# GpSimd's last-level products of near tokens: eight instructions of 384 elements in place of two of 1536

## The chip, the cores and the metric

The kernel runs on one core of a Trainium2 chip. The metric is the device time of one execution in microseconds (us); the time of a kernel is the median of its runs. TensorE appears in the profile as PE (matmuls) and PEld (weight loads), VectorE as DVE, ScalarE as ACT, GpSimd as POOL, and SyncE, which issues most DMAs, as SP.

## The reference

Two blocks follow each other. The first is a recurrence over 768 tokens for 4 sequences and 8 heads of 48 dimensions; the second is a feed-forward block over the 3072 tokens that come out of it (384 to 2048 to 384 dimensions). All is float32.

```python
for t in range(S):
    cur = einsum('bhd,bhe->bhde', u[None] * k_t, v_t)
    y[:, :, t] = einsum('bhd,bhde->bhe', r_t, state + cur)
    state = w_t[..., None] * state + einsum('bhd,bhe->bhde', k_t, v_t)
h = x @ w_in                      # x: y with the heads side by side
g = h * erf(softplus(h))
out = g @ w_out
```

Token t thus sees every earlier token s with the weight (sum over d of r[t,d] k[s,d] times the product of w between them).

## The kernel before, in words

**Steps.** The work is cut into 12 steps (s = 0 to 11) of 2 sequences by 128 tokens by 8 heads. Within a step, the weights between tokens are found by levels: at level n, blocks of 2^n tokens are split in two halves, and each token of the right half meets each token of the left half. Levels 5 and 6 are matmuls (`level_products`). For steps 5 to 11 the levels 1 to 4, the "near" tokens within a block of 16, are done without TensorE: `prepare(s)` holds r, k and w of the step as rows (128 partitions, each one block of 16 tokens by 48 dimensions), multiplies r by k elementwise, and sums over the 48 dimensions.

**`prepare(s + 1)` runs inside step s.** It is a generator; `attend_late(s, ...)`, the body of steps 5 to 11, advances it piece by piece between its own instructions, and step 4 (`attend`) does so for step 5. So the near tokens of steps 5 to 11 are prepared in steps 4 to 10, seven times in all. The names in `prepare`: `multiply(engine, level)` forms the products of a level (lines 484 to 493), `fade` multiplies r or k by decays (line 462), `add_total` forms decays over longer stretches (line 455), `sum_up` sums products over the 48 dimensions on VectorE (line 528).

**Level 4** has 8 left tokens by 8 right tokens by 48 dimensions for each partition: 3072 products. `multiply_last(nc.gpsimd, part)` (line 502) forms them on GpSimd, half of the left tokens at a time. Part 0 goes into the buffer `front`, which the profile shows as `rk`; part 1 goes into `back`, shown as `words` (r and k themselves lie in a `words` buffer too). Part 1 takes the place of the products of level 3, so it comes behind `sum_up(3)`. After part 1, GpSimd fades k for the last time (`fade(nc.gpsimd, k, 4)`, line 462). VectorE sums the two parts much later in the step (`sum_up(4, 0)` and `sum_up(4, 1)`, line 528 with 1536 elements), and SyncE then writes the faded k and the sums to DRAM and reads them back in another order (`k_blocks`, `by_blocks`, `by_tokens`, `kT`).

**The order of the work is written out by hand.** All engines run under `manual_schedule`, each in program order. What goes between the pieces of a late step is a string of tokens; for steps 6 to 10 it is

```python
USUAL = (
    "s P", "m", "ey P m s P P ep P", "m k22y P F P k11p F", "S1", "S2 S3 H k12y S4 H F",
    "s H ey m H H F s H ep H H",
)
```

for the places "front", "near", 0, 1, 2, 3, 4. `P` is an eighth of the output product of step s - 3 (`project_fast`, matmuls of line 1212, then sums on VectorE in lines 1232 and 1237), `H` a piece of the hidden product of step s - 1 (`hidden`, matmuls of line 1097, copied out by ACT in line 1106), `s`, `e` and `m` are softplus, erf and the multiplication `h <- h * erf` (VectorE, line 1062), `F` advances `prepare(s + 1)`, and `S`, `k` blend tokens for a later `P`. Step 5 has a list of its own, in which the output product is `project` (line 1129).

On VectorE, in steps 6 to 10, this gives the following row around the two GpSimd instructions of line 502: `sum_up(2)` (line 528), a multiplication `m` (1062, `h<-h,pp`), `sum_up(3)` (528), `kT` times the spread decays (793), a second `m` (1062, `h<-h,y`), the scaling of `in` by decays for level 5 (`scale`, line 333, 512 elements), a third `m` (1062, `h<-h,pp`), the sum `o<-o,m` (1232), `scale` for level 6 (333, `in<-in,w`), the sum `o<-o,m` (1237), two further `scale` (333).

The matmuls of `P` and of `H` share two PSUM buffers `m`. The first `H` of a step writes into the buffer that the VectorE instruction of line 1232 reads last. On TensorE it comes behind `state_part` (line 734, `pp<-v,kT`), which in its turn is behind the last `P`.

Of the kernel before, what the change touches and what calls it, by code (L numbers as in the profile page):

```python
# [17 lines left out]
P = 128  # L18
# [28 lines left out]
def view(ap, offset, dims):  # L47

    return bass.AP(ap.tensor, ap.offset + offset, [ap.ap[0], *dims])
# [12 lines left out]
def kernel(  # L62
# [18 lines left out]
    NH, D = v.shape[2:]  # L81
# [277 lines left out]
    def prepare(s):  # L359
# [3 lines left out]
        if s < DIRECT:  # L363
            rk1 = att.tile([P, 2, JP, C], FP32, name="rk1", bufs=1)
            ready[s] = (rk1,)
            parts = 1 if s else NJ
# [56 lines left out]
        else:  # L423
            half = view(tots[NEAR_LOG + 1], 1, [[2, NC], [C >> NEAR_LOG + 1, JP]])
# [3 lines left out]
            to = over_blocks[:].rearrange("p (h b) n -> p b h n", h=NC)  # L428
# [5 lines left out]
        r, k, w = rows_of.pop(s)  # L434
# [32 lines left out]
        for level in (0, 1, 2, 3):  # L467
            half = 1 << level - 1 if level else 0
# [5 lines left out]
        half = 1 << NEAR_LOG - 1  # L474
        parts = [x[:, : half * half * D // 2] for x in (front, back)]
# [22 lines left out]
        def multiply_last(engine, part):  # L498

            rows = half // 2  # L500
            left = k[:, part * rows : (part + 1) * rows]
            engine.tensor_mul(  # L502
                parts[part].rearrange("p (s t d) -> p s t d", t=half, d=D),
                r[:, None, half:].to_broadcast([P, rows, half, D]),
                left[:, :, None, :].to_broadcast([P, rows, half, D]),
            )

        def sum_up(level, part=None):

# [39 lines left out]
        if levels == NEAR_LOG:  # L549
            fade(beside, k, 3)  # L550
            add_total(beside, 3)
            fade(nc.vector, r, 3)
            sum_up(2)
            multiply_last(nc.gpsimd, 0)
            yield
            sum_up(3)
            multiply_last(nc.gpsimd, 1)
            fade(nc.gpsimd, k, NEAR_LOG)
        else:
            yield  # L560
            sum_up(2)
            sum_up(3)
# [917 lines left out]
    for kk in range(KT):  # L1480
        n = D // KT
        to, of = (x.rearrange("p (e m) -> p e m", e=NE) for x in (apart[:, kk], ident[:]))
        nc.vector.tensor_copy(out=to[:, :, D:], in_=of[:, :, kk * n : (kk + 1) * n])
    load_first()
    with tc.manual_schedule(
# [74 lines left out]
        s = n_steps  # L1560
# [108 lines left out]
```

## Time and profile before

| What | Value |
|---|---|
| Median of 3 runs | 584.71 us (583.98 to 586.29) |
| The profiled execution | 582.61 us |
| its span | 580.8 us |
| granted TensorE clock | 1.0 |
| PE busy | 572.0 us (98%) |
| DVE busy | 435.8 us (75%) |
| ACT busy | 355.4 us (61%) |
| POOL busy | 226.5 us (39%) |
| line 502, part 0 | 7 instructions of 1536 elements, mean 3447 ns |
| line 502, part 1 | 7 instructions of 1536 elements, mean 4201 ns |

The profile is of one execution. Its span runs from the first to the last instruction; the rest of its time, 1.8 us, lies around the span. In the timeline each row has the start in us from the span's start, the duration in us, the engine, the line, the operation, the tile that is written and those that are read, the shape, and, in brackets, how long the engine was idle before and who released it. Rows of one engine overlap by up to 0.1 us, because an instruction is recorded from its own start to its last write. A step of the kind 6 to 10 takes 44.87 us; the examples below are mostly from step 6 (235.75 to 280.62 us).

### The profile page before, as it was taken

To read this page: it belongs to the slowest core of one execution; us is meant where nothing else is said; L and a number is where in the kernel's file an instruction comes from. 1 tells how busy PE (TensorE), PEld (TensorE's weight loads), DVE (VectorE), ACT (ScalarE), POOL (GpSimd) and SP (SyncE) were. 2 spreads that over 40 slices of the span, in tenths; PEclk is the share of its full clock that TensorE was granted. 3 is DMA by queue.
4 is the path that set the end of the run, shared out by engine and by line. 5 is a ranking of instruction groups with operands and counts; after the bars stand their busy time and mean duration, and the time that the engine had idled before them with its cause. 6 is when DMAs were issued, how large, how long until landed. Compare 5 with 4: busy or idle time off the path is not lost.

```text
span 580.8 us, 16457 instructions
## 1 busy us (share of the span) xinstructions
PE 572.0 (98%) x7240; PEld 491.4 (85%) x7240; DVE 435.8 (75%) x462; ACT 355.4 (61%) x478; POOL 226.5 (39%) x222
## 2 busy tenths in 40 slices
PE   8999999999999999999999999999999999999997
PEld 6688886688578668998998998998898899988997
DVE  8784866998895798798699599599599537256640
ACT  3768787554453797847747747756666761388700
POOL 4566481606764675373273183173172000000000
PEclk9999999999999999999999999999999999999999
DMA  7595753250352326136135235234232301000000
GB/s 259 194 359 197 249 191 139 101 151 7 140 193 56 107 75 168 18 138 183 30 132 183 39 133 183 39 123 150 47 110 81 47 8 37 1 1 2 28 27 28
DMA packets 54080, 63.23 MB, mean 109 GB/s; under 512 B 35160, under 2 KB 40568, under 8 KB 52984
## 3 DMA queue, kind: packets, MB, share of 16 engines
q1 hardware_dynamic: 53624, 61.98, 33.7%
q8 instruction: 57, 0.93, 0.7%
q10 hardware_dynamic: 384, 0.20, 0.1%
q14 instruction: 15, 0.12, 0.1%
HBM read 52.39 MB, written 8.69 MB: 105 GB/s over the span
## 4 chain that ended last, share of the span: by engine, by line
PE 70%; issue 12%; DVE 12%; POOL 4%; DMA 1%; ACT 1%; SPq 0%; DVEq 0%; POOLq 0%; ACTq 0%
PE m L1097 30%; PE m L1212 12%; PE m L1129 11%; PE pp L627 5%; PE pp L1300 4%; DVE h L1062 3%; PE y L1300 2%; DVE sums L528 2%; POOL words L462 2%; DVE in L333 2%; DVE words L493 2%; POOL own L455 1%; PE y L659 1%; PE pp L734 1%; PE y L685 1%
## 5 line engine op out<-in xcount | busy, mean ns | idle before, releaser
L1097 PE MATMUL m<-xT,w_in_sb 128*128 128x256 f32 x960 | 214.6, 382 | 2.5 <-DVE o L1232 2.5
L1097 PEld LDWEIGHTS m<-xT,w_in_sb 128*128 128x128 f32 x960 | 180.0, 190 | 28.0 <-DVE o L1232 3.2
L333 DVE TENSOR_TENSOR in<-in,tot_sb 128x1024 f32<-128x1024 f32 (+1 forms) x55 | 79.7, 1449 | 16.4 <-PE pp L627 15.1
L1106 ACT COPY h<-m 128x512 f32<-128x512 f32 x80 | 46.3, 580 | 52.3 <-PE m L1097 52.3
L1129 PE MATMUL m<-w_out_sb,h 128*128 128x384 f32 x192 | 64.3, 491 | 0.0
L1129 PEld LDWEIGHTS m<-w_out_sb,h 128*128 128x128 f32 x192 | 35.7, 190 | 23.5 <-POOL w_out_sb L288 0.2
L1212 PE MATMUL m<-mixed,h 128*128 128x192 f32 x256 | 45.6, 331 | 0.0
L1212 PE MATMUL m<-w_out_sb,h 128*128 128x192 f32 x256 | 44.8, 329 | 0.0
L1212 PEld LDWEIGHTS m<-mixed,h 128*128 128x128 f32 x256 | 41.4, 190 | 0.9
L1057 ACT ACT_TABLE_LOAD x30 | 38.5, 1283 | 5.8 <-DVE h L1062 5.4
L1212 PEld LDWEIGHTS m<-w_out_sb,h 128*128 128x128 f32 x256 | 41.6, 190 | 0.3
L1212 PE MATMUL m<-w_out_sb,room 128*128 128x192 f32 x240 | 41.5, 326 | 0.0
L1053 ACT ACT_TABLE_LOAD x30 | 38.5, 1283 | 2.5 <-issue 2.0
L627 PEld LDWEIGHTS pp<-in 48*48 48x48 f32 (+4 forms) x2368 | 30.1, 120 | 11.5 <-issue 6.3
L1212 PEld LDWEIGHTS m<-w_out_sb,room 128*128 128x128 f32 x240 | 39.4, 190 | 0.0
L462 POOL TENSOR_TENSOR words<-words,own 128x384 f32<-128x384 f32 x21 | 28.7, 1367 | 22.5 <-DVE words L493 12.8
L627 PE MATMUL pp<-in 48*48 48x32 f32 (+4 forms) x2368 | 33.9, 206 | 0.0
L455 POOL TENSOR_TENSOR own<-rest 128x384 f32<-128x384 f32 x7 | 9.7, 1392 | 60.3 <-ACT o L1218 48.8
L1170 ACT COPY y<-h 128x1024 f32<-128x1024 f32 x12 | 12.2, 1018 | 34.2 <-DVE h L1062 25.1
L528 DVE TENSOR_REDUCE sums<-rk 128x16 f32<-128x768 f32 (+2 forms) x31 | 31.7, 1022 | 0.0
L1053 ACT ACTIVATE room<-h 128x1024 f32<-128x1024 f32 x28 | 29.6, 1059 | 0.3
L502 POOL TENSOR_TENSOR words<-words 128x1536 f32<-128x1536 f32 x7 | 29.4, 4201 | 0.0
(204 smaller groups left out, 996.6 us busy)
## 6 DMA issues: line engine op xcount, KB each, us to landing
in<-in_rkw SPq DMA_DIRECT2D x8, 1024.0 KB, 5.2
words<-in_moe_w_in SPq DMA_DIRECT2D x16, 384.0 KB, 5.0
words<-in_moe_w_out SPq DMA_DIRECT2D x16, 384.0 KB, 5.9
words<-in_rk_rows SPq DMA_DIRECT2D x8, 768.0 KB, 5.7
w<-in_rkw SPq DMA_DIRECT2D x11, 512.0 KB, 6.2
v<-in_v SPq DMA_DIRECT2D x12, 384.0 KB, 5.5
out<-o SPq DMA_DIRECT2D x23, 192.0 KB, 1.9
in<-in_rkw SPq DMA_DIRECT2D x7, 512.0 KB, 5.1
```

Source lines behind the costliest of these rows:

```text
L333: nc.vector.tensor_mul(halves, halves, view(tots[level - 1], 0, [[1, n], [2, nb], [0, half]]))
L462: engine.tensor_mul(to, to, of[:, :, None, :].to_broadcast([P, NEAR // 2 // half, half, D]))
L502: engine.tensor_mul(parts[part].rearrange("p (s t d) -> p s t d", t=half, d=D), r[:, None, half:].to_broadcast([P, rows, half, D]), left[: ...
L528: nc.vector.tensor_reduce(out=to, in_=of, axis=mybir.AxisListType.X, op=ALU.add)
L627: nc.tensor.matmul(to, lhsT=rk(1, n)[rows(e), s0 : s0 + m], rhs=right, start=True, stop=True,)
L1053: nc.scalar.activation(sp_room, chunks[0], AF.Softplus)
L1057: nc.scalar.activation(at, sp_room, AF.Erf)
L1097: nc.tensor.matmul(ps[:, ff, :], lhsT=w_in_sb[:, g * FG + f + ff, kk * P : (kk + 1) * P], rhs=xT[:, kk, :], start=kk == 0, stop=kk == KT - 1,)
L1106: nc.scalar.copy(h[:, f : f + FT, :], ps[:])
L1129: nc.tensor.matmul(ps[j][:], lhsT=gs[g][:, f, j * C : (j + 1) * C], rhs=w_out_sb[:, g * FG + f, :], start=g + f == 0, stop=g == NG - 1 and ...
L1212: nc.tensor.matmul(to, lhsT=a[:, f], rhs=b[:, f], start=start and f == 0, stop=f == FG - 1, skip_group_check=True,)
L1300: nc.tensor.matmul(to[:, e], lhsT=a[:, 2 * i + e], rhs=b, start=start and not k, stop=True, skip_group_check=True,)
```

## The change

Line 502 and the lines around it: in place of one instruction for half of the left tokens (4 left tokens by 8 right tokens by 48), each left token has an instruction of its own (8 right tokens by 48 dimensions, 384 elements). The 8 right tokens are read as one run of 384 elements, and the row of k is repeated for each of them. The products, the places they are written to and their order on GpSimd are the same. With it, GpSimd is given 4 instructions for part 0 and 4 for part 1 in each of the seven preparations, 56 in place of 14.

```diff
         def multiply_last(engine, part):
 
             rows = half // 2
-            left = k[:, part * rows : (part + 1) * rows]
-            engine.tensor_mul(
-                parts[part].rearrange("p (s t d) -> p s t d", t=half, d=D),
-                r[:, None, half:].to_broadcast([P, rows, half, D]),
-                left[:, :, None, :].to_broadcast([P, rows, half, D]),
-            )
+            to = parts[part].rearrange("p (s t d) -> p s t d", t=half, d=D)
+            for i in range(rows):
+                engine.tensor_mul(
+                    to[:, i], r[:, half:],
+                    k[:, part * rows + i, None].to_broadcast([P, half, D]),
+                )
```

## The prediction

> **What bounds the kernel now.** I read the page's busy times first, then who TensorE waited for, then the timeline of TensorE, VectorE and GpSimd around line 502.
>
> ```profile
> PE 572.0 (98%) x7240; PEld 491.4 (85%) x7240; DVE 435.8 (75%) x462; ACT 355.4 (61%) x478; POOL 226.5 (39%) x222
> ```
>
> TensorE is the bound: 98% busy, at clock 1.0, and in program order. GpSimd is far from it. So the change can gain only what TensorE still loses to waiting, and can cost only by making TensorE wait. Its waits:
>
> ```profile
> PE m L1097 <- DVE o L1232: 2.5, 5, 0.5
> PEld m L1097 <- DVE o L1232: 3.2, 5, 0.7
> ```
>
> Columns: us in total, times, longest. It is one stall in each of five steps (6 to 10): the first hidden matmul waits for VectorE's line 1232 to free its PSUM buffer. TensorE's timeline shows its size, in step 5 without the stall and in step 6 with it:
>
> ```profile
> 213.48 0.94 PE L734 MATMUL pp<-v,kT 64*48 64x48 f32 x64
> 214.34 20.99 PE L1097 MATMUL m<-xT,w_in_sb 128*128 128x256 f32 x96
> ```
>
> ```profile
> 257.78 0.94 PE L734 MATMUL pp<-v,kT 64*48 64x48 f32 x64
> 259.22 20.99 PE L1097 MATMUL m<-xT,w_in_sb 128*128 128x256 f32 x96 [0.51 <-DVE o L1232]
> ```
>
> From line 734's start to line 1097's: 0.86 us free, 1.44 us stalled, so 0.58 us are lost per step. Why is VectorE late? Its timeline in step 6, then GpSimd's:
>
> ```profile
> 249.06 1.21 DVE L1062 TENSOR_TENSOR h<-h,pp 128x1024 f32<-128x1024 f32 x1
> 250.19 1.74 DVE L528 TENSOR_REDUCE sums<-words 128x32 f32<-128x1536 f32 x1
> 251.85 1.86 DVE L793 TENSOR_TENSOR kT<-kT,spread 128x768 f32<-128x768 f32 x1
> 253.64 1.21 DVE L1062 TENSOR_TENSOR h<-h,y 128x1024 f32<-128x1024 f32 x1
> 254.77 2.80 DVE L333 TENSOR_TENSOR in<-in,tot_sb 128x512 f32<-128x512 f32 x1
> 257.49 1.21 DVE L1062 TENSOR_TENSOR h<-h,pp 128x1024 f32<-128x1024 f32 x1
> 258.62 0.54 DVE L1232 TENSOR_TENSOR o<-o,m 128x384 f32<-128x384 f32 x1
> ```
>
> ```profile
> 249.46 3.44 POOL L502 TENSOR_TENSOR rk<-words 128x1536 f32<-128x1536 f32 x1
> 252.87 4.16 POOL L502 TENSOR_TENSOR words<-words 128x1536 f32<-128x1536 f32 x1
> 257.10 1.33 POOL L462 TENSOR_TENSOR words<-words,own 128x384 f32<-128x384 f32 x1
> 264.84 0.84 POOL L813 TENSOR_TENSOR faded<-middle,tot_sb 128x384 f32<-128x384 f32 x1 [6.40 <-DVE middle L810]
> ```
>
> The same two VectorE instructions in step 11, where GpSimd has nothing to do:
>
> ```profile
> 465.09 0.95 DVE L793 TENSOR_TENSOR kT<-kT,spread 128x768 f32<-128x768 f32 x1
> ...
> 476.62 0.69 DVE L333 TENSOR_TENSOR in<-in,tot_sb 128x512 f32<-128x512 f32 x1 [6.46 <-PE pp L627]
> ```
>
> Line 793 takes 0.95 alone and 1.86 in step 6; line 333 takes 0.69 alone and 2.80. Both end a fixed time after a GpSimd instruction does: line 502's part 1 ends at 257.03, line 333 at 257.57, 0.54 later; part 0 ends at 252.90, line 793 at 253.71, 0.81 later. And part 1, which starts at 252.87, takes 0.72 longer than part 0, about line 793's 0.81. So a VectorE instruction with both inputs in SBUF and a GpSimd multiplication take turns, each holding the other off for its whole length. Instructions with an input in PSUM (line 1062: 1.21) and reductions (line 528: 1.74) run at their usual length beside line 502. VectorE thus loses 1.86 - 0.95 = 0.9 and 2.80 - 0.69 = 2.1 us, 3.0 in all, before line 1232, five times as much as the stall it causes.
>
> **The change, part by part.** *One small instruction.* The trace has no GpSimd multiplication of this exact form. The nearest rows of 384 elements, undisturbed, in step 4:
>
> ```profile
> 148.49 0.99 POOL L455 TENSOR_TENSOR own<-rest 128x384 f32<-128x384 f32 x1
> 149.45 0.99 POOL L462 TENSOR_TENSOR words<-words,rest 128x384 f32<-128x384 f32 x1
> ```
>
> From start to start 0.96. The row of line 813 (0.84) is the low end; the longest usual row of 384, 1.41 (line 455 at 240.19, with a turn of VectorE's inside), the high one. I take 0.96. Eight are 7.7 us against 2 x 3.41 = 6.8 (part 0 to part 1, start to start): GpSimd has 0.9 us more per step (from -0.1 to +4.5 by the ends).
>
> What a start costs by rows: line 455 takes 0.35 for 96 elements and 0.58 for 192 (start to start at 249.11 and 245.35), so 2 x 0.35 - 0.58 = 0.12 is fixed; six more starts are 0.7 us.
>
> [...]
>
> *What hides that.* GpSimd is idle for 6.40 us before line 813. With turns for lines 793 (0.81), 333 (0.54) and perhaps two more of line 333 (1.13 each), the eight and the last fade end at 249.46 + 7.7 + 3.6 + 0.86 = 261.6, not 258.43. Who needs them: SP issues `k_blocks` (the faded k) at 262.68; VectorE sums the parts at 268.07 and 269.73. At 1.41 each, the end is 265.2: `k_blocks` is 2.6 late, but its copy back is issued only at 273.69 and it lands in 6.7, so 4.3 us are spare there; line 813 is 0.4 late, and its reader, line 816, runs at 271.39. No cost. Past these covers it would cost us for us.
>
> *What goes.* I replay step 6 with pieces of 0.96 from 249.46: they end at 250.42, 251.38, 252.34. Line 793 can start when line 528 ends, 251.94; it waits to 252.34 and ends at 253.15. The `m` (1.13) ends at 254.28. GpSimd's fourth and fifth pieces end at 254.11 and 255.07; line 333 waits from 254.28 to 255.07 and ends at 255.61; the next `m` at 256.74, line 1232 (0.54) at 257.28, not 259.16. Line 1097 could start at 257.78 + 0.86 = 258.64 at the earliest. So VectorE is 1.4 us early and the stall of 0.58 goes. At worst both waits are a whole piece: 251.94 + 0.96 + 0.81 + 1.13 + 0.96 + 0.54 + 1.13 + 0.54 = 258.0, still in time. With pieces of 1.41 it is 258.9, and 0.3 of the 0.58 goes.
>
> *What is late next.* Nothing on TensorE: behind 734 it has 1097, whose second PSUM buffer is freed by line 1237 by about 260 and wanted 2.6 us after 1097's start. `own` (line 589) is ready at 277.60 for line 659 at 280.14, which moves up by 0.58. In steps 4 and 5 VectorE also loses turns, but TensorE has no wait there. After step 10 line 502 does not occur.
>
> *Sum.* 5 x 0.58 = 2.9 us. Profiled: 582.61 - 2.9 = 579.7, span 577.9. The median is 2.1 above the profiled execution: 584.71 - 2.9 = **581.8**, 0.5% less. About 0.5% is also what a measurement of this kernel can tell from no change.
>
> **Rivals.** *The run of small instructions keeps VectorE out.* If GpSimd's next piece always takes the turn before the waiting VectorE does, line 793 waits for four pieces (253.30) and ends at 254.11, line 333 waits for the other four (257.95), and line 1232 ends at 260.1: 0.9 later in five steps, 4.7 us, 589.4. If all eight hold together, line 793 ends at 257.95 and line 1232 at 261.2: 2.05 x 5, 595.0. It decides from the point where the two waits pass today's 3.0 us. For it: turns are not always given. At 183.13 GpSimd's line 407 (1.04 alone) took 5.95 while VectorE ran four two-input instructions in a row. Against it: GpSimd's line 462 and line 1017 follow each other at 167.80 with no pause, and VectorE's waiting line 333 still came between them (line 1017 took 1.82, not 0.84).
>
> *The stall stays, or goes in part*: pieces dearer than 1.41, or some other wait beneath it: 583 to 584.7.
>
> *GpSimd becomes late*: from some 2.2 us a piece (249.46 + 8 x 2.2 + 2.5 = 269.6) the sum at 269.73 waits, then 8 us per step for each us more: at 2.5 it is 2.4 us in each of five steps, up to 597. No row of 384 is near that (at most 1.88, a turn included).
>
> **Chances.** Stall gone, 581.8: 0.74. Since 2.9 us lies on the bound of 0.5% (2.92), this case is split: 0.50 beyond it, because what delays VectorE further in the longer of the timed runs would sit in the same stall, and 0.24 within. In part or not at all: 0.09, within 0.5%. VectorE kept out, 0.14, and GpSimd late, 0.03: slower. The range takes in the first two with the spread of the runs shown (-0.7, +1.6): 580.2 to 585.2; only the slower 0.17 is left out.
>
> **What would show it.** After: no wait of line 1097 for line 1232; 0.86 from 734 to 1097 in steps 6 to 10, which take 44.3; line 333 (512 elements) under 1.7 us in all steps, line 793 under 1.9; pieces 0.84 to 1.0 when undisturbed; line 813 still waiting for line 810. Wrong: the wait grows (VectorE kept out), or 1097 waits for another.

## The result and the profile after

The median fell from 584.71 us to 581.62 us (580.42 to 581.88, 4 runs); the ratio is 0.994 with a 95% interval of 0.9915 to 0.9964. The forecast was 581.8. The profiled execution fell less, from 582.61 to 581.53 us (span 580.8 to 579.7), for a reason that has nothing to do with the change and is taken up below.

A correction to the description of the kernel first: of VectorE's scalings in line 333, the one of 512 elements belongs to level 6 of the step itself, and `in<-in,w` and the two after it to levels 1 to 3 of the next step. Their places in the row, which is what the prediction uses, are as described.

Who TensorE waited for, after (us in total, times, longest). The five waits for VectorE's line 1232 are gone from the list:

```profile
PE m L934 <- POOL ident masks.py:199: 1.7, 1, 1.7
PE pp L943 <- DVE own L637: 0.6, 2, 0.4
PE m L1097 <- ACT h L1106: 0.3, 1, 0.3
```

TensorE's timeline in step 6, which lies 1.83 us later than in the execution of before:

```profile
259.61 0.94 PE L734 MATMUL pp<-v,kT 64*48 64x48 f32 x64
260.47 20.99 PE L1097 MATMUL m<-xT,w_in_sb 128*128 128x256 f32 x96
```

0.86 us from line 734 to line 1097, the unstalled distance, with no idle time in brackets. VectorE and GpSimd in the same step:

```profile
253.69 1.33 DVE L793 TENSOR_TENSOR kT<-kT,spread 128x768 f32<-128x768 f32 x1
254.95 1.21 DVE L1062 TENSOR_TENSOR h<-h,y 128x1024 f32<-128x1024 f32 x1
256.08 1.31 DVE L333 TENSOR_TENSOR in<-in,tot_sb 128x512 f32<-128x512 f32 x1
257.32 1.21 DVE L1062 TENSOR_TENSOR h<-h,pp 128x1024 f32<-128x1024 f32 x1
258.45 0.54 DVE L1232 TENSOR_TENSOR o<-o,m 128x384 f32<-128x384 f32 x1
```

```profile
251.29 4.60 POOL L503 TENSOR_TENSOR rk<-words 128x384 f32<-128x384 f32 x4
255.85 5.31 POOL L503 TENSOR_TENSOR words<-words 128x384 f32<-128x384 f32 x4
261.24 1.86 POOL L462 TENSOR_TENSOR words<-words,own 128x384 f32<-128x384 f32 x1
265.86 0.83 POOL L813 TENSOR_TENSOR faded<-middle,tot_sb 128x384 f32<-128x384 f32 x1 [2.75 <-DVE middle L810]
```

Line 793 took 1.33 and not 1.86, line 333 took 1.31 and not 2.80, while GpSimd's two halves took 4.60 and 5.31 and not 3.44 and 4.16: VectorE's turns now fall inside them. GpSimd's idle time before line 813 shrank from 6.40 to 2.75. Line 1232 ended at 258.99, 1.48 us before line 1097 started; before, line 1097 started 0.06 us after it ended (259.16 and 259.22). The busy times of one step (us, and instructions, for each engine):

```profile
237.09:281.39 44.30, 44.30 (x533) 40.63 (x533) 37.42 (x38) 31.44 (x39) 22.93 (x26) 1.00 0.39 117
```

The step takes 44.30 us instead of 44.87, and by the records TensorE (the first busy time) is busy through all of it: no wait is left in these steps that could be taken away.

### The profile page after: what moved, and what is told of

It is laid out like the page before. It is cut to its first block, busy times and chain, and to the rows that moved or that the text cites. A ratio compares the mean times of both kernels' runs of the same rounds, so it can differ in the third digit from the quotient of the medians.

```text
span 579.7 us, 16499 instructions
## 1 busy us (share of the span) xinstructions
PE 572.8 (99%) x7240; PEld 492.2 (85%) x7240; DVE 429.0 (74%) x462; ACT 354.8 (61%) x478; POOL 244.8 (42%) x264
## 4 chain that ended last, share of the span: by engine, by line
PE 95%; DVE 1%; POOL 1%; DMA 1%; issue 1%; ACT 0%; SPq 0%; DVEq 0%; POOLq 0%; ACTq 0%
PE m L1097 35%; PE m L1212 28%; PE m L1129 11%; PE pp L627 5%; PE pp L1300 4%; PE y L1300 2%; PE y L659 2%; PE y L685 2%; PE pp L734 2%; PE m L934 1%; DMA words<-in_moe_w_in 1%; PE pp L943 1%; PE pp L1010 1%; POOL tot_sb L355 0%; PE pp L1212 0%
## 5 line engine op out<-in xcount | busy, mean ns | idle before, releaser
L333 DVE TENSOR_TENSOR in<-in,tot_sb 128x1024 f32<-128x1024 f32 (+1 forms) x55 | 76.4, 1389 | 16.9 <-PE pp L627 15.5
L1106 ACT COPY h<-m 128x512 f32<-128x512 f32 x80 | 46.3, 579 | 59.7 <-PE m L1097 59.7
L462 POOL TENSOR_TENSOR words<-words,own 128x384 f32<-128x384 f32 x21 | 30.7, 1462 | 22.8 <-DVE words L493 13.1
L503 POOL TENSOR_TENSOR words<-words 128x384 f32<-128x384 f32 x28 | 39.7, 1447 | 0.0
L503 POOL TENSOR_TENSOR rk<-words 128x384 f32<-128x384 f32 x28 | 32.4, 1186 | 0.0
```

The lines of the kernel that those rows point to most:

```text
L333: nc.vector.tensor_mul(halves, halves, view(tots[level - 1], 0, [[1, n], [2, nb], [0, half]]))
L462: engine.tensor_mul(to, to, of[:, :, None, :].to_broadcast([P, NEAR // 2 // half, half, D]))
L503: engine.tensor_mul(to[:, i], r[:, half:], k[:, part * rows + i, None].to_broadcast([P, half, D]),)
L1106: nc.scalar.copy(h[:, f : f + FT, :], ps[:])
```

## The experiments

The theory is that of the prediction: a VectorE instruction with two SBUF inputs and a GpSimd multiplication take turns, so what VectorE loses is the rest of the GpSimd instruction that is running (0.9 us in line 793 and 2.1 in line 333 before); line 1232 is late by the sum of two such waits; the change shortens them. The rivals were that finer work is better as such (A), that only executions were compared (B), that the wait of line 793 for part 0 is what counts (C), that the small form itself is faster (D). In the first three experiments line numbers behind the edit are shifted by 3 or 14. The first four kernels ran on one chip beside 31 runs of before (median 584.01, 582.94 to 587.43), the last three on one beside 19 (583.80).

**Four instructions of 768**, against the changed kernel.

```diff
-            for i in range(rows):
-                engine.tensor_mul(
-                    to[:, i], r[:, half:],
-                    k[:, part * rows + i, None].to_broadcast([P, half, D]),
-                )
+            n = 2
+            for i in range(0, rows, n):
+                left = k[:, part * rows + i : part * rows + i + n]
+                engine.tensor_mul(
+                    to[:, i : i + n],
+                    r[:, None, half:].to_broadcast([P, n, half, D]),
+                    left[:, :, None, :].to_broadcast([P, n, half, D]),
+                )
```

> GpSimd gets four instructions of 768 elements (two left tokens each). Theory (turns: a VectorE instruction with two SBUF inputs waits for the GpSimd instruction that is running, so only the length of one instruction counts): with 1.77 us each, worked out between 0.957 for 384 and 3.41 for 1536, line 793 waits to 253.0 and line 333 (512 elements) to 255.5 of step 6 of the kernel before, line 1232 ends at 257.7, before 258.64; the stall of 0.58 us goes in all five steps as with eight, ratio to before 0.994 to 0.996, about 581.7 us. Rival A (gain in proportion to how finely the work is cut): half of it, ratio 0.997 to 0.998. Rival B (what was measured is a difference between executions, not between kernels): 1.000.

581.0 us, ratio 0.9948 [0.9929, 0.9968]: the whole gain with half the instructions. VectorE and GpSimd in step 6 (796 is line 793 of before):

```profile
252.34 2.00 DVE L796 TENSOR_TENSOR kT<-kT,spread 128x768 f32<-128x768 f32 x1
...
255.40 1.18 DVE L333 TENSOR_TENSOR in<-in,tot_sb 128x512 f32<-128x512 f32 x1
```

```profile
249.94 3.59 POOL L505 TENSOR_TENSOR rk<-words 128x768 f32<-128x768 f32 x2
253.49 4.77 POOL L505 TENSOR_TENSOR words<-words 128x768 f32<-128x768 f32 x2
```

Line 793 took longer than with eight (2.00 against 1.33) and line 333 a little less (1.18 against 1.31), and the stall was gone from all five steps. Only the margin differs, and it does not show in the time. Rivals A and B fall: A's 0.997 lies only just outside the interval, but A leaves half of the stall, and the trace has none. One instruction of 768 took 1.78 us from start to start, against 1.77 worked out.

**Part 0 alone cut**, against the kernel before (the instructions that each call gives out are written beside it).

```diff
-            multiply_last(nc.gpsimd, 0)      # one of 1536
+            multiply_last(nc.gpsimd, 0)      # four of 384
             multiply_last(nc.gpsimd, 1)      # one of 1536, as before
```

> Only part 0 is cut into four of 384; part 1 stays one instruction of 1536. Theory of turns: line 793 gets its turn 0.5 us earlier, but part 1 then starts at 254.0 and not 252.9, ends at 257.4, and line 333, which waits for its end, with it; line 1232 ends at 259.6, 0.46 later than before, so the stall grows from 0.58 to 1.04 and five steps lose 2.3 us: ratio 1.004, about 587.0 us, slower than before. Rival A (finer is better, any part): ratio 0.997. Rival C (the wait of line 793 for part 0 is what counts): ratio 0.995.

586.18 us, ratio 1.0036 [1.002, 1.0051]: slower than before, as the theory of turns alone had it. VectorE, GpSimd and TensorE in step 6 (the lines 807, 333 and 1246 are 793, 333 and 1232 of before, 513 and 502 are parts 0 and 1, 748 and 1111 are 734 and 1097):

```profile
254.97 1.33 DVE L807 TENSOR_TENSOR kT<-kT,spread 128x768 f32<-128x768 f32 x1
...
257.35 3.75 DVE L333 TENSOR_TENSOR in<-in,tot_sb 128x512 f32<-128x512 f32 x1
...
262.15 0.54 DVE L1246 TENSOR_TENSOR o<-o,m 128x384 f32<-128x384 f32 x1
```

```profile
252.56 4.60 POOL L513 TENSOR_TENSOR rk<-words 128x384 f32<-128x384 f32 x4
257.12 3.43 POOL L502 TENSOR_TENSOR words<-words 128x1536 f32<-128x1536 f32 x1
```

```profile
260.89 0.94 PE L748 MATMUL pp<-v,kT 64*48 64x48 f32 x64
262.75 5.45 PE L1111 MATMUL m<-xT,w_in_sb 128*128 128x256 f32 x24 [0.92 <-DVE o L1246]
```

Line 793 got its turn early (1.33), exactly as with eight. But that turn, and the dearer part 0, moved part 1 to 257.12. This execution lies 3.10 us later than that of before (part 0 starts at 252.56 and not 249.46), so part 1 came 1.15 us later within the step, and line 333 0.52 earlier; line 333 met part 1 near its start and waited for nearly all of it: it took 3.75 us, against 2.80 before. TensorE's idle time grew from 0.51 to 0.92. From line 734 of step 5 to that of step 11 the trace has 270.54 us against 268.43 before: 2.1 us lost, against 2.3 worked out. Rivals A and C, which had this as a gain, fall.

**Part 1 alone cut**, likewise.

```diff
             multiply_last(nc.gpsimd, 0)      # one of 1536, as before
-            multiply_last(nc.gpsimd, 1)      # one of 1536
+            multiply_last(nc.gpsimd, 1)      # four of 384
```

> Only part 1 is cut into four of 384; part 0 stays one instruction of 1536. Theory of turns: line 793 waits as before (ends 253.7), line 333 waits to 255.5 and not to 257.0, line 1232 ends at 257.7, before 258.64: the whole gain, ratio 0.994 to 0.996, about 581.7 us. Rival A (finer is better, any part): half the gain, 0.997. Rival C (the wait of line 793 for part 0 counts): 1.000.

580.96 us, ratio 0.9957 [0.9937, 0.9978]: the whole gain. VectorE and TensorE in step 6 (lines shifted as in the run before):

```profile
252.26 1.87 DVE L807 TENSOR_TENSOR kT<-kT,spread 128x768 f32<-128x768 f32 x1
...
255.18 1.31 DVE L333 TENSOR_TENSOR in<-in,tot_sb 128x512 f32<-128x512 f32 x1
```

```profile
258.18 0.94 PE L748 MATMUL pp<-v,kT 64*48 64x48 f32 x64
259.05 5.23 PE L1111 MATMUL m<-xT,w_in_sb 128*128 128x256 f32 x23
```

Line 793 took 1.87, as before, line 333 took 1.31, and no wait for line 1232 is left (line 1097 starts 0.87 us after line 734). The gain of the change is thus its second half; the first half alone costs 2 us.

**The scaling moved, GpSimd as before.**

```diff
         take_level(own, pp, LOG)
-        scale(s, LOG)
         run(1, following)
+        scale(s, LOG)
```

> The two instructions of 1536 of the kernel before are kept; only VectorE's line 333 of 512 elements is moved behind the work of place 1 (behind the third multiplication, lines 1232 and 1237, and two scalings). Theory of turns: nothing with two SBUF inputs stands between line 793 and line 1232 any more, so line 1232 ends at 256.4 and the stall of 0.58 goes without any change on GpSimd: ratio 0.994 to 0.996, about 581.7 us. Rival D (the small instructions themselves make GpSimd or VectorE faster): 1.000, and the wait of line 1097 for line 1232 stays.

580.97 us, ratio 0.9948 [0.9933, 0.9964]. The same gain with GpSimd's two instructions of 1536 left alone. VectorE in step 6, and GpSimd's part 1 beside it:

```profile
255.32 1.21 DVE L1062 TENSOR_TENSOR h<-h,y 128x1024 f32<-128x1024 f32 x1
256.45 1.21 DVE L1062 TENSOR_TENSOR h<-h,pp 128x1024 f32<-128x1024 f32 x1
257.58 0.54 DVE L1232 TENSOR_TENSOR o<-o,m 128x384 f32<-128x384 f32 x1
```

```profile
254.54 4.18 POOL L502 TENSOR_TENSOR words<-words 128x1536 f32<-128x1536 f32 x1
```

Between line 793 and line 1232 there are only instructions with an input in PSUM now; they run at 1.21 and 0.54 right through part 1, and line 1232 is done at 258.12, while line 734 starts at 259.46. Rival D falls as what the gain needs: nothing on GpSimd had to become faster.

**Each small instruction twice.** The second of each pair writes the same products again, so that GpSimd's time in these lines doubles at the same length of one instruction; the diff is against the changed kernel.

```diff
-            for i in range(rows):
+            for i in [i for i in range(rows) for _ in range(2)]:
```

> Each of the eight small instructions is given out twice in a row (the second writes the same products again): GpSimd's time in these lines doubles, at the same length of one instruction. Theory (turns, and GpSimd's time under cover): line 1232 is as early as with eight, the stall stays away; the last fade ends at about 270 of step 6 of the kernel before, the faded k goes out 7.6 us later than in the kernel before, but nothing that TensorE needs is late: ratio to before 0.994 to 0.997, 581.7 to 583 us. Rival (GpSimd's time counts): 8 us more in each of seven preparations, ratio 1.05 or more.

581.76 us, ratio 0.9964 [0.9948, 0.9979]. GpSimd is busy for 309.1 us against 244.8 with eight, about 9 us more per preparation, and the gain is still there. The sum over part 1 is now just late, and line 813 no longer waits for anybody:

```profile
271.31 1.75 DVE L528 TENSOR_REDUCE sums<-words 128x32 f32<-128x1536 f32 x1 [0.37 <-POOL words L503]
```

```profile
261.23 10.05 POOL L503 TENSOR_TENSOR words<-words 128x384 f32<-128x384 f32 x8
...
272.32 0.84 POOL L813 TENSOR_TENSOR faded<-middle,tot_sb 128x384 f32<-128x384 f32 x1
```

The cover that VectorE's sum gives thus ends here, at 2 x 0.96 = 1.9 us for each of the eight products. TensorE does not wait yet: it loses nothing in steps 6 to 10.

**Each small instruction three times**, with `range(3)` in the same place.

> Each small instruction is given out three times in a row. Theory: the cover is gone. Part 1 ends at about 277 of step 6 of the kernel before, the sum over it, due at 269.7, waits 7.4 us, so the weights between near tokens (line 589) are ready at about 285 and TensorE's line 659, due at 279.6, waits some 5.5 us in each of five or six steps: ratio 1.035 to 1.06, 605 to 620 us. If the cover were larger than was read from the profile, the ratio would stay below 1.01.

623.92 us, ratio 1.0682 [1.0652, 1.0712]: slower, as expected, but by more than the expected 605 to 620. In step 7 VectorE waits for part 1, and TensorE for what VectorE does behind that sum:

```profile
345.14 1.75 DVE L528 TENSOR_REDUCE sums<-words 128x32 f32<-128x1536 f32 x1 [8.85 <-POOL words L503]
...
347.48 1.21 DVE L1062 TENSOR_TENSOR h<-h,y 128x1024 f32<-128x1024 f32 x1
```

```profile
348.75 0.66 PE L659 MATMUL y<-own,v 64*48 64x64 f32 x32 [2.17 <-DVE h L1062]
```

VectorE's wait, worked out as 7.4, was 62.8 us in seven preparations, 9.0 each. TensorE's wait is not the one that was expected:

```profile
PE y L659 <- DVE h L1062: 11.7, 5, 2.6
PE pp L627 <- DVE in L333: 8.9, 7, 3.7
```

Line 659 writes the PSUM buffer `y` that line 1062 reads, and line 1062 stands behind the late sum on VectorE. It does not wait for the new weights of line 589, as the expectation had it: in step 7 it starts at 348.75, and VectorE's rows up to 352 do not have line 589 yet, for the `own` that it reads there was prepared a step earlier. VectorE was 8.85 us late and TensorE waited 2.17 (2.6 at the longest of five such waits), so behind the sum there is a second cover of some 6 to 7 us. TensorE's idle time grew by 24.1 us in all (31.0 against 6.9 after), against the 27.5 that were priced (5.5 in each of five steps). And the page's line of the granted TensorE clock, full in the profiles of before and after, has dips from slice 13 on:

```profile
PEclk9999999999998999899799899899989989999999
```

The mean granted clock was 0.975 (1.0 in all other traces here), and TensorE was busy for 591.2 us against 572.8 after, with the same 7240 matmuls. The expectation had priced TensorE's waits alone; of the 42.5 us by which the span is longer than after, these 18.4 are not waits, and without them the time would have been at the lower end of what was expected. Stretches of 529 to 535 matmuls were busy for 46.3 to 46.8 us at a clock of 0.97 and for 48.05 to 48.29 at 0.93, against 44.3 for the 533 of a step after, at 1.0. A clock lower by 0.025 over 591.2 us is worth about 15 us (an estimate, with busy time taken as one over the clock), so it accounts for most of the 18.4 and not for all.

**Both edits.** Eight small instructions and the moved scaling.

> Both: the eight small instructions, and line 333 of 512 elements moved as in the run with the scaling moved. Theory: each alone takes the whole stall away and TensorE has no other wait in these steps, so together they give what each gives: ratio 0.994 to 0.996, about 581.7 us. Rival (two separate gains): 0.990.

581.56 us, ratio 0.9959 [0.9946, 0.9971]: no more than either alone. One stall can be taken away once. None of these kernels beats the changed one; three reach the same time.

## Why the prediction held, point by point

**The stall as the whole stake.** The prediction took 5 x 0.58 = 2.9 us. From line 734's start in step 5 to that in step 11, the trace of before has 268.43 us; the runs with four instructions and with part 1 alone cut have 265.54, 2.89 less, and the changed kernel 265.69, 2.74 less. Shown by taking the stall away in three different ways, with the same gain each time. That the median came within 0.2 us of the forecast is partly luck: the interval of the ratio stands for a gain of 2.1 to 5.0 us, and the forecast started from 584.71, while the 31 and the 19 other runs of before have medians of 584.01 and 583.80. The reason given for a gain beyond 0.5%, that the longer of the timed runs hold more of the stall, was not tested. The stated range does not come out of its own terms: 581.8 less 0.7 is 581.1, and 584.7 plus 1.6 is 586.3, not 580.2 and 585.2; the measured time lies in both.

**Taking turns.** The replay of step 6 gave the ends 253.15 (line 793), 255.61 (line 333) and 257.28 (line 1232); measured, less the 1.83 us by which the step starts later, 253.19, 255.56 and 257.16. In the trace after, the pieces of part 0 start at 251.29, 252.25, 253.21 and 254.17; the first three take 0.99 to 1.00 and the fourth 1.72, with line 793's turn inside. The experiments with one part cut separate the two waits: it is the wait for part 1 that made line 1232 late, and that wait depends on where in part 1 line 333 arrives.

**The small instruction.** Taken at 0.96 us from start to start; measured 0.96 undisturbed. Eight less two of 1536 are 8 x 0.957 - 2 x 3.41 = 0.84 us more, against 0.9 predicted; the sum of rows of line 455 was 0.7. That sum was too low because it set a distance between starts (0.35) beside a duration (0.58: GpSimd's next instruction starts only at 247.77, after a wait). By durations on both sides, 2 x 0.38 - 0.58 = 0.18, less the 0.04 by which rows overlap, 0.14 is fixed, and six starts are 0.84. The run with four of 768 has the same price of a start: two pieces of 384 less one of 768 are 2 x 0.957 - 1.775 = 0.14 us. The price was no reason against the change here, since GpSimd had the time.

**The cover.** Less the same 1.83 us, the last fade, predicted to end at 261.6, ended at 261.27. Line 813 kept 2.75 us of idle time. `k_blocks` was issued at 261.30, right behind the fade, and still earlier than the 262.68 of before, since the issues ahead of it on SyncE follow line 1237, which is earlier. One reading was wrong: `own` of line 589, "ready at 277.60 for line 659 at 280.14", is not what line 659 reads there. Line 659 reads an `own` prepared a step earlier and writes the buffer that line 1062 reads (as the run with each instruction three times shows); line 1062 ends at 273.07, 6.5 us before line 659 is due without the stall. Nothing was late either way, so the forecast did not suffer.

**The rivals.** VectorE was not kept out: its waiting instruction came between two of GpSimd's in each of the steps 6 to 10 (line 793 took 1.33 and line 333 1.31 in all five). The rival of a late GpSimd had its threshold at 2.2 us a piece; the run with each instruction twice shows it at 1.9. The term that was off is the turns inside the run, counted as 2.5 us there; they are five (0.81, 0.54 and three of 1.13), 4.7 in all, which puts 249.46 + 8p + 4.7 = 269.73 at p = 1.95. What the rival then charged, "8 us per step for each us more", was wrong as well: behind the sum VectorE's lateness has the second cover, so an estimate from these rows is that TensorE begins to wait for the late sum at about 2.8 us a piece (1.95 + 6.5 / 8); at 2.5 that wait would have cost nothing.

**Where the profiled execution differs.** It was forecast at 579.7 and took 581.53. At line 734 of step 5 it was already 1.67 us behind the profiled execution of before (215.15 against 213.48), nearly all of it by 66 us, long before the changed code first runs. The nine profiled executions (all kernels of this document) differ by 3.1 us already at line 734 of step 3, before the changed code first runs (134.36 before, 136.03 after, 137.47 with part 0 alone cut). So it varies from one execution to the next; the medians of several runs are less open to it.

**What stays open.** In step 5 the changed kernel lost 0.16 us: line 1097 waited once for ACT's line 1106, ACT being some 0.7 us behind TensorE there. The run with the moved scaling lost 0.27 in that step, the ones with each twice and with both edits 0.6, those with four instructions and with part 1 alone cut nothing. Whether this belongs to a kernel or to an execution was not settled.

## What to carry to other kernels

When an instruction takes about as much longer as the rest of another engine's running instruction lasts, look for turns. Here the price was set by the length of one instruction of the other engine and by the moment of arrival, and not by the other engine's total time as long as that stayed covered: with twice the work the gain stayed (0.9964), with three times the kernel took 6.8% more than before. So cut the instruction that the critical engine arrives behind, in the place where it arrives; cutting the one ahead of it can shift the other into the way (part 0 alone: 1.0036). Or reorder the critical engine so that nothing that takes turns stands ahead of what the bound engine waits for; and size the gain by the bound engine's stall (0.58 us a step), not by the waits that go (about 2 us).

## What the runs showed of the hardware

GpSimd's pieces of 384 follow each other with an overlap of some 0.04 us in the records after (0.99 to 1.00 long, 0.96 from start to start; why records overlap was not tested), and VectorE's waiting instruction was let in between them all the same, in each of the steps 6 to 10; yet in the trace of before GpSimd's line 407 took 5.95 us, 4.9 more than the 1.04 alone, while four VectorE instructions ran in a row (from 183.56, and likewise from 137.53). Elsewhere in that trace the two engines alternate (VectorE's line 333 and GpSimd's lines 462 and 1017, 166 to 171), so who is let in when both wait stays open, and so does why line 407, whose record starts 0.43 us before the first of the four, did not hold that one off. VectorE's lines 1062 and 1232, with one input in PSUM, and its reductions over 1536 elements (line 528) kept their lengths beside GpSimd's: 1.21, 0.54 and 1.74, within 0.02, through the traces of before and after, and the same in step 6 or 7 of the six other runs whose VectorE rows are given above. And where TensorE waited repeatedly, with three instructions in place of each, its granted clock was 0.93 to 0.97 in five stretches of 49 to 53 us, each with about the matmuls of a step that takes 44.3 (the longest waits in that trace were 2.6 us at line 659 and 3.7 at line 627), and 18.4 of the 42.5 us lost are longer busy time for the same matmuls, not waits. That the waits made the clock fall is argued from their coming together, not tested by itself.
